# Reading a guard flag ahead of the last stores, and ending a program without a barrier

## The chip, the cores and the metric

The kernel runs on one core of a Trainium2 chip. A core has five engines with instruction streams of their own: TensorE (PE in the profile; its weight loads are PEld), VectorE (DVE), ScalarE (ACT), GpSimd (POOL) and SyncE (SP), which here only issues transfers. ACT issues some of the last stores too. The engines keep order among themselves by semaphores. The time of a run is the device's, in microseconds (us). The profile is of one execution; its span runs from the first to the last instruction that is recorded for the kernel.

## The reference

Attention with pairs of queries averaged, then a two-branch layer with a maximum of the two, for 8 batches and 8 heads, in float32:

```python
q_pool = q.reshape(B, H, S // 2, 2, D).mean(axis=3)          # S = 1152, D = 64
scores = (1 / sqrt(D)) * matmul(q_pool, k.transpose(0, 1, 3, 2))
scores = scores - max(scores, axis=-1, keepdims=True)
attn = exp(scores)
attn = attn / (sum(attn, axis=-1, keepdims=True) + 1e-09)
attn_out = matmul(attn, v)
x = attn_out.transpose(0, 2, 1, 3).reshape(4608, 512)
out = maximum(x @ w1, x @ w2) @ w_out                        # 512 -> 1024 -> 512
```

## The kernel before

The whole program is written out as one straight line for each engine. A planner (`Plan`) collects operations with what they read and write; hand-written strings (`pe_order`, `dve_order`, `pool_order`, `sp_order`) then set the order on each engine, and `solve` works out which operation has to wait for which. `emit` (line 187 on) runs through the operations of one engine, puts the waits in front of each and issues it.

The softmax is computed without subtracting the row's maximum. That is only sound while the sums of the exponentials stay within 1e-18 to 1e18, so the kernel tests this while it runs and has a second, slow way of computing everything for the case that they do not. The test works on the reciprocals of all sums, kept in `rcs`: two reductions and two comparisons on DVE (lines 1544 to 1548) leave one number in each of the 128 partitions, a small transfer on SP (line 1550) turns that column into a row, `badr`, and a last reduction on DVE (line 1551) leaves one integer, `flag`. It is zero when all is well.

When an engine has issued the last of its operations, it waits until the flag is written (the count `sure` on DVE's semaphore) and loads the flag from memory into a register of its own (`reg_load`, line 1594; in the profile a TENSOR_LOAD). Then comes `guarded` (line 219 on): `If_ne(taken, 0)` is a compare and branch on every engine. With a zero flag it jumps over the slow way. Behind it stands `landed()`: SP waits until every store to the output has landed, one wait for each of the eight semaphores of stores (`d_o0` to `d_o3` for those that SP issued, `d_z0` to `d_z3` for ACT's; line 207). The program ends with a barrier over all engines (line 1603), in which each reports and is released by GpSimd.

The end of the computation, around which the change lies: SP's last operations in `sp_order` are `g`, which is the small transfer of the flag, and seven `o`, stores of output tiles of 128 rows. Each tile is stored in two halves, one issued by SP and one by ACT (line 865). The tiles are copied out of TensorE's result banks by ACT (lines 1021 and 1006) and by DVE (lines 1024 and 1010); the last tile is split into 384 and 128 columns. ACT has in its last twelve operations one relu (line 908), four such copies and its seven stores. DVE has three copies after the flag.

Of the kernel before, what the change touches and what calls it, by code (L numbers as in the profile page):

```python
# [19 lines left out]
class Plan:  # L20
# [166 lines left out]
    def sems(self):  # L187
        return list(self.INORDER), sorted(self.dma_total)

    def emit(self, eng, h, sem, last_waits=()):  # L190
        for o in self.ops:
            if o["eng"] != eng:
                continue
            todo = {}
            for d in o["waits"]:
                p = self.ops[d]
                key = p["dma"] if p["dma"] is not None else p["eng"]
                todo[key] = max(todo.get(key, 0), p["count"])
            for key, v in todo.items():
                h.wait_ge(sem[key], v)  # L200
            inst = o["fn"](h)
            if o["dma"] is not None:
                inst.then_inc(sem[o["dma"]], 16)
            elif o["inc"]:
                inst.then_inc(sem[eng], 1)
        for key in last_waits:
            h.wait_ge(sem[key], self.dma_total[key])
# [132 lines left out]
def bass_funnel_attn__then__act_maxout2_kernel(  # L340
# [38 lines left out]
    with outer:  # L379
# [41 lines left out]
        plan = Plan()  # L421
# [741 lines left out]
        def landed(kind, i):  # L1163
            if (kind, i) not in loaded:
                return False
            return plan.ops[loaded[kind, i]]["seen"] <= now() + 0.5
# [421 lines left out]
        sem = {n: ctx.enter_context(nc.semaphore("sem_" + n)) for n in engines + dmas}  # L1588
        taken = nc.alloc_registers("taken")
        sure = [o["count"] for o in plan.ops if "gd4" in o["w"]][0]  # L1590
        for name, h in (("POOL", nc.gpsimd), ("SP", nc.sync), ("DVE", nc.vector), ("ACT", nc.scalar), ("PE", nc.tensor)):
            plan.emit(name, h, sem)
            h.wait_ge(sem["DVE"], sure)
            h.reg_load(taken[h.engine], flag[0:1, 0:1])
        room.close()
        stored = [f"d_o{s}" for s in range(4)] + [f"d_z{s}" for s in range(4)]

        def landed():
            plan.emit("-", nc.sync, sem, last_waits=stored)

        guarded(nc, taken, landed, q, k, v, moe_w1, moe_w2, moe_w_out, out)
        landed()
        nc.all_engine_barrier()


# [26 lines left out]
```

## Time and profile before

| | us |
|---|---|
| median of 3 runs | 367.5 (366.64, 367.50, 372.56) |
| the profiled execution | 368.65 |
| its span | 366.94 |
| PE busy | 355.2 (97%) |
| ACT busy | 315.0 (86%) |
| DVE busy | 242.2 (66%) |
| flag written (start of its reduction) | 351.04 |
| last matmul group starts | 360.69 |

The busy time of an engine is a sum over its instructions in the span. Reading of registers, branches, semaphores and the issuing of transfers are not counted as busy, so an engine that goes through the end of the program shows as idle there; such steps are found under their source lines instead, with their durations in ns (least, median, most) and the first and last start in us.

### The profile page before, as it was taken

To read this page: it belongs to the slowest core of one execution; us is meant where nothing else is said; L and a number is where in the kernel's file an instruction comes from. 1 tells how busy PE (TensorE), PEld (TensorE's weight loads), DVE (VectorE), ACT (ScalarE), POOL (GpSimd) and SP (SyncE) were. 2 spreads that over 40 slices of the span, in tenths; PEclk is the share of its full clock that TensorE was granted. 3 is DMA by queue.
4 is the path that set the end of the run, shared out by engine and by line. 5 is a ranking of instruction groups with operands and counts; after the bars stand their busy time and mean duration, and the time that the engine had idled before them with its cause. 6 is when DMAs were issued, how large, how long until landed. Compare 5 with 4: busy or idle time off the path is not lost.

```text
span 366.9 us, 13339 instructions
## 1 busy us (share of the span) xinstructions
PE 355.2 (97%) x5945; PEld 222.7 (61%) x5945; DVE 242.2 (66%) x526; ACT 315.0 (86%) x355; POOL 124.6 (34%) x111
## 2 busy tenths in 40 slices
PE   8898999999999999999999999999999999999993
PEld 6675555666564666656565665666666556666842
DVE  2777468877589767948957595676976856624511
ACT  4999989989999999999989999999999989893311
POOL 1245995344046322552251612623524420100000
PEclk9999999999999999999999999999999999999998
DMA  7999999999869996996997999997998662724015
GB/s 249 404 397 394 404 291 313 224 300 297 218 122 270 297 296 189 252 264 177 290 266 212 283 252 285 271 275 182 287 214 212 161 161 50 153 45 94 13 39 141
DMA packets 77791, 84.78 MB, mean 231 GB/s; under 512 B 50080, under 2 KB 50848, under 8 KB 77728
## 3 DMA queue, kind: packets, MB, share of 16 engines
q1 hardware_dynamic: 77168, 83.09, 84.9%
q8 instruction: 48, 0.79, 0.9%
q10 hardware_dynamic: 560, 0.79, 0.6%
q14 instruction: 15, 0.12, 0.1%
HBM read 62.91 MB, written 9.44 MB: 197 GB/s over the span
## 4 chain that ended last, share of the span: by engine, by line
PE 92%; ACT 4%; DMA 1%; issue 1%; SPq 0%; POOL 0%; DVE 0%; DVEq 0%
PE sps L714 20%; PE sps L625 12%; PE sps L961 11%; PE fb L961 10%; PE fb L625 9%; PE sps L928 9%; PE fb L928 7%; ACT et L721 4%; PE sps L994 3%; PE sps L637 2%; PE fb L846 2%; PE fb L637 2%; PE fb L994 1%; PE sps L901 1%; DMA kraw<-in_k_dram 1%; PE fb L901 1%
## 5 line engine op out<-in xcount | busy, mean ns | idle before, releaser
L721 ACT ACTIVATE et<-sps 128x1024 bf16<-128x1024 f32 (+1 forms) x336 | 307.0, 1005 | 21.7 <-PE sps L714 19.7
L714 PE MATMUL sps<-qpT,kT 64*128 64x256 bf16 (+7 forms) x1162 | 118.3, 283 | 0.3 <-DVE kT L601 0.2
L579 DVE STREAM_TRANSPOSE qpT<-qp 32x288 bf16<-32x288 bf16 x216 | 101.4, 469 | 5.6 <-PE sps L714 1.5
L714 PEld LDWEIGHTS sps<-qpT,kT 64*128 64x128 bf16 x1162 | 48.0, 94 | 47.5 <-ACT et L721 15.5
L519 POOL TENSOR_TENSOR qp<-qraw 128x576 bf16<-128x576 f32 x30 | 42.1, 1406 | 96.0 <-DVE qpT L579 79.4
L525 POOL TENSOR_SCALAR vE<-vraw 128x1152 bf16<-128x1152 f32 x32 | 36.8, 1151 | 60.4 <-DMA vraw<-in_v_dram 57.8
L625 PE MATMUL sps<-vE,et 128*128 128x65 bf16 x1368 | 48.4, 193 | 0.0
L625 PEld LDWEIGHTS sps<-vE,et 128*128 128x128 bf16 x1368 | 43.6, 97 | 6.0 <-issue 5.3
L486 POOL TENSOR_SCALAR kbf<-kraw 128x1152 bf16<-128x1152 f32 x31 | 35.6, 1150 | 33.0 <-DMA kT<-kbf 17.0
L928 PE MATMUL sps<-xT,wd 64*128 64x512 bf16 (+3 forms) x368 | 43.4, 326 | 0.0
L961 PE MATMUL sps<-wo,stage 64*128 64x512 bf16 x256 | 36.8, 376 | 0.0
L625 PE MATMUL fb<-vE,et 128*128 128x65 bf16 x936 | 33.5, 193 | 1.1 <-issue 1.1
L625 PEld LDWEIGHTS fb<-vE,et 128*128 128x128 bf16 x936 | 29.9, 97 | 6.1 <-issue 5.3
L928 PE MATMUL fb<-xT,wd 64*128 64x512 bf16 (+3 forms) x272 | 33.5, 333 | 0.1
L961 PE MATMUL fb<-wo,stage 64*128 64x512 bf16 x224 | 33.0, 376 | 0.0
L937 DVE TENSOR_SCALAR stage<-sps 128x1024 bf16<-128x1024 f32 (+3 forms) x23 | 22.3, 969 | 15.4 <-PE sps L928 15.2
L937 DVE TENSOR_SCALAR stage<-fb 128x1024 bf16<-128x1024 f32 (+3 forms) x17 | 17.0, 999 | 10.7 <-PE fb L928 10.4
L928 PEld LDWEIGHTS sps<-xT,wd 64*128 64x128 bf16 x368 | 15.6, 94 | 13.4 <-PE sps L928 1.4
L647 DVE RECIPROCAL rcs<-sps 128x5 f32<-128x5 f32 (+1 forms) x38 | 7.0, 184 | 19.8 <-PE sps L625 19.3
L961 PE MATMUL sps<-w,xT 64*128 64x512 bf16 x128 | 18.7, 376 | 0.0
L972 DVE COPY stage<-sps 128x1024 f32<-128x1024 f32 x8 | 9.8, 1224 | 12.8 <-PE sps L961 12.7
L961 PEld LDWEIGHTS sps<-wo,stage 64*128 64x128 bf16 x256 | 12.1, 94 | 9.5
(86 smaller groups left out, 293.8 us busy)
## 6 DMA issues: line engine op xcount, KB each, us to landing
vraw<-in_v_dram SPq DMA_DIRECT2D x32, 576.0 KB, 6.4
kraw<-in_k_dram SPq DMA_DIRECT2D x31, 576.0 KB, 6.6
qraw<-in_q_dram SPq DMA_DIRECT2D x31, 576.0 KB, 6.6
out_dram<-stage SPq DMA_DIRECT2D x21, 256.0 KB, 5.5
out_dram<-stage SPq DMA_DIRECT2D x23, 128.0 KB, 2.9
xT<-in_moe_w_dram SPq DMA_DIRECT2D x4, 512.0 KB, 10.8
stage<-in_moe_w_out_dram SPq DMA_DIRECT2D x4, 512.0 KB, 13.8
stage<-in_moe_w_dram SPq DMA_DIRECT2D x4, 512.0 KB, 13.6
```

The costliest lines, as they stand in the source:

```text
L486: op("POOL", lambda g: g.tensor_scalar(kbf[s][:, :, :, :].rearrange("p t h d -> p h t d"), kraw[r][:, :, :, :], 1.0, 1.0, ALU.mult, ALU.mu ...
L519: op("POOL", lambda g: g.tensor_tensor(qpf[s][:, :, :], qraw[r][:, :, 0, :], qraw[r][:, :, 1, :], ALU.add), r=[f"qraw{r}"], w=[f"qp{s}.0", ...
L525: op("POOL", lambda g: g.tensor_scalar(vE[r][:, :, :, 0:D].rearrange("p t h d -> p h t d"), vraw[r][:, :, :, :], 1.0, 1.0, ALU.mult, ALU.m ...
L579: op("DVE", lambda e: e.transpose(view[dst:dst + 32, :, 32 * pb:32 * pb + 32], qpf[s][src:src + 32, :, 32 * db:32 * db + 32]), r=[f"qp{s}. ...
L625: last = e.matmul(fb[m][:, sb * 66:sb * 66 + 65], et[:, a:a + P], vE[vs][:, t, half, 0:65], start=(t == 0), stop=(t == NT - 1))
L637: last = e.matmul(fb[m][rows(half), NCH * 66:NCH * 66 + 65], et[:, a:a + NB], vE[vs][:, t, half, 0:65], start=(t == 0), stop=(t == NT - 1))
L714: last = e.matmul(sps[r][:, h, col:col + hi - lo], kT[i % 3][rows(h), t, :], qpT[i % 3][rows(h), lo:hi], start=True, stop=True)
L721: op("ACT", lambda e: e.activation(et2[:, :, c:c + z - a], sps[r][:, :, a - g * W:z - g * W], EXP, scale=scale), r=[f"s{r}"], w=keys + ([f ...
L928: last = e.matmul(fb[m + k][:, 0:size], wd[z, ct, (f0 + k) * P:(f0 + k + 1) * P], xT[z, ct, n0:n1], start=(turn == 0 and ct == 0), stop=(t ...
L937: dve(lambda e: e.tensor_scalar_max(gT[:, f0:f0 + 2, g0:g0 + size], wide[m // 2][:, :, 0:size], 0.0), [f"f{m}", f"f{m + 1}"], w + [f"f{m}" ...
L961: last = e.matmul(fb[m + k][:, :], lhs, rhs, start=(turn == 0 and j == 0), stop=(turn == 1 and j == NC_ + NF - 1))
L994: return e.matmul(fb[m][:, 0:c1 - c0], lhs, rhs[:, c0:c1], start=(j == 0), stop=(j == NC_ + NF - 1))
```

## The change

Three things change, and nothing in the computation.

1. `emit` gets an argument `extra`: a number and a function, which is called in front of the operation that has so many operations of this engine left, itself included. The wait for the flag and the load into the register become a function `look`. On SP it is called before the last 7 operations, on ACT before the last 12, on DVE before the last 3; on POOL and PE behind the last one, as it was. The branch stays where it was on all engines.
2. The eight waits of `landed()` are put in the order in which the last operations of their semaphores stand in the plan, in place of the order of their names.
3. The barrier over all engines at the program's end is left out.

```diff
-    def emit(self, eng, h, sem, last_waits=()):
-        for o in self.ops:
-            if o["eng"] != eng:
-                continue
+    def emit(self, eng, h, sem, last_waits=(), extra=None):
+        mine = [o for o in self.ops if o["eng"] == eng]
+        for n, o in enumerate(mine):
+            if extra is not None and n == len(mine) - extra[0]:
+                extra[1](h)
             todo = {}
...
         sure = [o["count"] for o in plan.ops if "gd4" in o["w"]][0]
-        for name, h in (("POOL", nc.gpsimd), ("SP", nc.sync), ("DVE", nc.vector), ("ACT", nc.scalar), ("PE", nc.tensor)):
-            plan.emit(name, h, sem)
+
+        def look(h):
             h.wait_ge(sem["DVE"], sure)
             h.reg_load(taken[h.engine], flag[0:1, 0:1])
+
+        early = {"SP": 7, "ACT": 12, "DVE": 3}
+        for name, h in (("POOL", nc.gpsimd), ("SP", nc.sync), ("DVE", nc.vector), ("ACT", nc.scalar), ("PE", nc.tensor)):
+            if name in early:
+                plan.emit(name, h, sem, extra=(early[name], look))
+            else:
+                plan.emit(name, h, sem)
+                look(h)
         room.close()
-        stored = [f"d_o{s}" for s in range(4)] + [f"d_z{s}" for s in range(4)]
+        place = {o["dma"]: n for n, o in enumerate(plan.ops)}
+        stored = sorted((f"d_{c}{s}" for c in "oz" for s in range(4)), key=lambda s: place[s])

         def landed():
             plan.emit("-", nc.sync, sem, last_waits=stored)

         guarded(nc, taken, landed, q, k, v, moe_w1, moe_w2, moe_w_out, out)
         landed()
-        nc.all_engine_barrier()
```

## The prediction

> **What bounds the kernel now.** I read the page first, then the chain that ended last near its end, then the timeline, the DMA issues and the lines of the last 16 us engine by engine. The page and the end of the chain:
>
> ```profile
> span 366.9 us, 13339 instructions
> PE 92%; ACT 4%; DMA 1%; issue 1%; SPq 0%; POOL 0%; DVE 0%; DVEq 0%
> 357.23 4.09 PE sps L994 x30
> 361.44 0.29 DVE stage L1010
> ```
>
> TensorE carries 92% of the chain, and the change touches none of its work. The chain that the profile draws ends with the last copy to `stage`, at 361.44 + 0.29 = 361.73. The span ends at 366.94 (the 366.9 of the page), so 5.2 us follow in which no engine computes. Everything the change can win lies there; what it can lose also lies in front of the tail's stores, where it puts three reads of the flag.
>
> The last transfers, from the timelines of SP and ACT (first pair), the line of the stores and the DMA issues (last pair: KB, us to landing):
>
> ```profile
> 360.19 2.67 SPq L865 DMA_DIRECT2D out_dram<-stage  x3
> 361.32 1.54 ACTq L865 DMA_DIRECT2D out_dram<-stage  x2
> L865 SPq DMA_DIRECT2D out_dram<-stage x7: 466/467/1037, 355.0 to 361.8; - x7
> L865 ACTq DMA_DIRECT2D out_dram<-stage x7: 497/498/1007, 355.0 to 361.9; - x7
> out_dram<-stage SPq DMA_DIRECT2D x1, 32.0 KB, 3.0
> out_dram<-stage ACTq DMA_DIRECT2D x1, 32.0 KB, 3.1
> ```
>
> Both queues finish issuing at 362.86 (360.19 + 2.67, 361.32 + 1.54). The last store begins to issue at 361.9 on ACT and lands 3.1 us later, at 365.0. So the output is complete at 365.0, and 1.9 us of the span lie behind that. What SP does meanwhile is in the rows of the flag, of line 207 (the waits on the stores, where the branch is also entered) and of line 1603 (the barrier):
>
> ```profile
> L1551 DVE TENSOR_REDUCE flag<-badr x1: 273/273/273, 351.0 to 351.0; 1x1 int32<-1x128 f32 x1
> L1594 POOLq TENSOR_LOAD <-flag x1: 487/487/487, 351.4 to 351.4; - x1
> L1594 PEldq TENSOR_LOAD <-flag x1: 613/613/613, 359.5 to 359.5; - x1
> L1594 DVEq TENSOR_LOAD <-flag x1: 628/628/628, 361.5 to 361.5; - x1
> L1594 ACTq TENSOR_LOAD <-flag x1: 986/986/986, 362.9 to 362.9; - x1
> L1594 SPq TENSOR_LOAD <-flag x1: 803/803/803, 362.9 to 362.9; - x1
> L207 SPq EVENT_SEMAPHORE  x4: 28/28/28, 366.4 to 366.6; - x4
> L207 POOLq COMPARE_BRANCH  x1: 45/45/45, 351.9 to 351.9; - x1
> L207 PEldq COMPARE_BRANCH  x1: 3712/3712/3712, 360.2 to 360.2; - x1
> L207 DVEq COMPARE_BRANCH  x1: 72/72/72, 362.1 to 362.1; - x1
> L207 SPq COMPARE_BRANCH  x1: 58/58/58, 363.8 to 363.8; - x1
> L207 ACTq COMPARE_BRANCH  x1: 54/54/54, 363.9 to 363.9; - x1
> L1603 POOLq DRAIN  x1: 107/107/107, 352.3 to 352.3; - x1
> L1603 PEldq DRAIN  x1: 73/73/73, 364.0 to 364.0; - x1
> L1603 ACTq DRAIN  x1: 79/79/79, 364.4 to 364.4; - x1
> L1603 DVEq DRAIN  x1: 57/57/57, 365.1 to 365.1; - x1
> L1603 SPq DRAIN  x1: 13/13/13, 366.7 to 366.7; - x1
> L1603 PEldq EVENT_SEMAPHORE  x1: 51/51/51, 366.9 to 366.9; - x1
> ```
>
> SP's path after its last issue is: flag load from 362.9 (0.80 us), branch at 363.8, then nothing until its first wait at 366.4. The landing at 365.0 is passed while SP is still between branch and wait. Four wait records from 366.4 to 366.6 therefore go through at their own pace; SP reaches the barrier at 366.7, last of the five engines, and the span ends 0.2 us later. The hole of 2.6 us between branch and first wait is the largest piece. POOL and ACT need 0.4 and 0.5 us from branch to next instruction (351.9 to 352.3, 363.9 to 364.4), DVE 3.0 (362.1 to 365.1), PE 3.8 (360.2 to 364.0). Blocks of instructions are fetched in just these holes. The DMA view, for 361 to 362.6, for 363.2 to 363.8, and for 364.5 to 365.3, in this order (queue, packets, MB, share of 16 engines):
>
> ```profile
> q8 instruction: 1, 0.02, 4.9%
> q14 instruction: 1, 0.01, 4.3%
> q14 instruction: 2, 0.02, 7.6%
> ```
>
> They took 0.049 x 16 x 1.6 = 1.25 us, 0.043 x 16 x 0.6 = 0.41 us, and together 0.076 x 16 x 0.8 = 0.97 us, some 0.5 each. By their times I give the first to PE, the second to DVE and one of the last to SP; that attribution is inferred.
>
> **The change part by part.** *The early reads.* SP's moves in front of its last seven instructions, the tail's stores; ACT's in front of its last twelve (one relu, four copies, seven stores); DVE's in front of its last three copies. No DMA moves. Each wait is for the flag, written at 351.0 + 0.27 = 351.3. Behind it are queued:
>
> ```profile
> SPq L865 <- ACT stage L1021: 7.4, 3, 5.3
> 354.08 0.38 ACT L908 ACTIVATE stage<-sps 128x256 bf16<-128x256 f32 x1 [5.17 <-PE sps L901]
> 355.54 0.69 DVE L1024 COPY stage<-fb 128x512 f32<-128x512 f32 x1 [4.22 <-PE fb L994]
> ```
>
> With the dearest load (ACT's 0.99) the read is over at 352.3. ACT next has work at 354.08, SP's first store issues at 355.0, after an idle stretch of up to 5.3 us, and DVE's copy starts at 355.54 after 4.22 idle. The covers are 1.8, 2.7 and 3.2 us, so I cost the early reads at nothing. Without its cover ACT's read would cost up to 1.0, once, as the relu at 354.08 feeds TensorE. PE and POOL read where they did.
>
> *What leaves SP's end.* The load goes from its path: the branch can stand where the load began, 362.9 in place of 363.8, a gain of 0.9 (0.80 and the gap beside it). There are two bounds. POOL's load, with nothing before it, took 0.49, SP's and ACT's, right behind a store's issue, 0.80 and 0.99; if the excess of 0.3 is the issue still draining, the branch may inherit it, and the gain is 0.6. The last issue took 1.04 against a median of 0.47, beside DVE's load (361.5 for 0.63), which also goes; if that load slowed it, the gain is up to 0.6 more. I take 0.9: the branches of SP, ACT, DVE and POOL, 45 to 72 ns whether behind a slow load or a quick one, show nothing that an issue could hold up.
>
> *The jump stays.* Only the read moves; the branch is still behind the last store. It then reaches its target at 362.9 + 2.6 + 0.06 = 365.6 instead of 366.4. That is still behind the landing at 365.0, by 0.5 us. So *the order of the waits* is worth nothing: all eight are fulfilled when SP arrives, and the four records cost their 0.2 to 0.3 us in either order. If the jump were short it would be worth at most three of the four records, 0.2.
>
> A rule of the Trainium skill speaks against hoping for more. The row: SP's 2.6 us against ACT's 0.5. The page Runtime: NRT & Kernel Launch, section Instruction fetch mechanics, says that only two pages are kept, fetched in sequence, and that a taken branch to a place outside them stalls until its page is fetched. By this rule the gap belongs to the target's distance and moves with the branch whole, which gives the sum below; by ACT's row alone SP would jump in 0.5 and the landing would decide, which is a rival.
>
> *No barrier.* From SP's 366.7 to the end at 366.94 are 0.2 us; they go. The other four engines then end by themselves; the latest of them, DVE, is at its barrier at 365.1 now, still before SP's new end, so none is late.
>
> The sum: 0.9 + 0.2 = 1.1 us. The profiled execution, 368.65 with a span of 366.94 and 1.7 around it, becomes 367.5, its span 365.8. Against the median of the three runs, 367.5, it is 366.4.
>
> **The rivals.** *The jump becomes short* (as on ACT and POOL). Then the last landing decides: 365.0 and a wait of 0.1, span 365.1, gain 1.8, time 365.7. For it: two engines jump in half a microsecond. Against it: SP's branch skips the same code as before, and nothing in the change shortens it.
>
> *The fetch queues behind the stores: slower.* SP's fetch now starts some 0.9 us earlier, near 363.9 instead of 364.7, and the DMA engines are then busier:
>
> ```profile
> 361.20:362.20 1.00, 0.10 (x2) 0.00 (x0) 0.29 (x1) 0.09 (x1) 0.00 (x0) 1.00 0.89 221
> 362.20:363.20 1.00, 0.00 (x0) 0.00 (x0) 0.00 (x0) 0.00 (x0) 0.00 (x0) 1.00 0.76 221
> 363.20:364.20 1.00, 0.00 (x0) 0.00 (x0) 0.00 (x0) 0.00 (x0) 0.00 (x0) 1.00 0.42 111
> 364.20:365.20 1.00, 0.00 (x0) 0.00 (x0) 0.00 (x0) 0.00 (x0) 0.00 (x0) 0.53 0.14 33
> ```
>
> Its columns end with the clock, the DMA share and GB/s. If the fetch had to wait until the stores are through (365.0) and then ran as long as PE's (1.25), it would end at 366.25. SP's first wait comes 1.2 us behind its fetch now (366.4 against 364.7 + 0.5), so it would come at 367.5, and the span would end near 367.7: 0.8 slower, time 368.3. It decides from the point where branch to first wait takes over 3.7 us (2.6 and the 1.1 won). For it: PE's 3.8, taken at a DMA share of 0.89. Against it: DVE's fetch ran at a share of 0.42 and took 0.41, no longer than SP's 0.5 in a quiet stretch.
>
> *The change doesn't do what it says*: the time of a run doesn't follow SP's last wait, because what lies around the span (1.7 us) takes up what the kernel's end gives. Then it is 367.5 again. For it: no record shows that part. Against it: it is counted from an end that moves. The Trainium skill (same page, section The ~15µs preamble/postamble breakdown) states that the runtime has a barrier of its own over all engines after the kernel; by that too only the kernel's own 0.2 would go.
>
> **How the numbers follow.** Forecast 0.63, short jump 0.10, queued fetch 0.12, nothing moved 0.12, others 0.03. The predicted time is the first's, 366.4. The range: downwards 365.7 of the short jump, less half of what the two nearer runs differ by (366.64 and 367.50, so 0.4), 365.3, and a tenth for the shorter last issue; upwards the queued fetch's 368.3. So 365.2 to 368.3. A bound of 2%, 7.4 us, is about what a measurement of this kernel can tell from no change (its three runs reach from 366.64 to 372.56). All 5.2 us behind the last copy would not reach it, and no rival does either: within 2% has 0.95, faster 0.02, slower 0.03, these for a disturbance that no row shows.
>
> **What would show it.** Right: flag loads of SP, ACT and DVE near 351.4; first tail store still at 355.0 and last copy at 361.4; SP's branch at 362.9, its first wait near 365.6 and all four records within 0.3; no line of the barrier; a span of 365.8. Wrong: a relu of ACT later than 354.1 (the read had no cover), a branch that starts late or lasts long (it inherited the load's time), a first wait before 365.0 (short jump) or after 366.4 (queued fetch), or a shorter span with the same time.

## The result, and the profile after

| | before | changed |
|---|---|---|
| median of 20 runs each, us | 368.68 (366.64 to 372.56) | 367.60 (366.59 to 373.14) |
| the profiled execution, us | 368.65 | 367.43 |
| its span, us | 366.94 | 366.20 |
| around the span, us | 1.71 | 1.24 |

The ratio of changed to before is 0.9963, 95% interval 0.9947 to 0.9979; it leaves out the few runs in a slower state (such as the one of 373.14), and so is not the quotient of the two medians. On 368.7 us that is 1.4 us less, between 0.8 and 2.0; the medians differ by 1.1.

The last computing steps of the changed kernel, from the timelines of ACT, DVE and SP (start us, length us, what):

```profile
353.71 0.38 ACT L909 ACTIVATE stage<-sps 128x256 bf16<-128x256 f32 x1 [5.17 <-PE sps L902]
350.66 0.27 DVE L1552 TENSOR_REDUCE flag<-badr 1x1 int32<-1x128 f32 x1 [1.99 <-DMA badr<-bad]
355.17 0.69 DVE L1025 COPY stage<-fb 128x512 f32<-128x512 f32 x1 [4.23 <-PE fb L995]
361.06 0.29 DVE L1011 COPY stage<-sps 128x128 f32<-128x128 f32 x1 [2.67 <-PE sps L995]
354.59 8.47 SPq L866 DMA_DIRECT2D out_dram<-stage  x7
```

Everything up to here is the old kernel 0.37 to 0.38 us sooner: the last copy starts at 361.06 in place of 361.44, and it lies as far behind the flag's reduction as before (10.40 us both times). So 0.37 us of the shorter span come from ahead of the tail, where the change does nothing, and the other 0.37 from the tail. The start of the last copy differs by more than that from execution to execution (360.2 to 362.6 over the kernels below), and so the tail is measured from there.

The flag, the branch with SP's waits, and the stores, from the lines of the source (ns least, median, most; first and last start in us):

```profile
L1595 SPq TENSOR_LOAD <-flag x1: 479/479/479, 351.0 to 351.0; - x1
L1595 ACTq TENSOR_LOAD <-flag x1: 477/477/477, 351.0 to 351.0; - x1
L1595 DVEq TENSOR_LOAD <-flag x1: 543/543/543, 351.0 to 351.0; - x1
L208 SPq EVENT_SEMAPHORE  x4: 28/28/28, 365.9 to 366.2; - x4
L208 PEldq COMPARE_BRANCH  x1: 4246/4246/4246, 359.8 to 359.8; - x1
L208 SPq COMPARE_BRANCH  x1: 54/54/54, 363.1 to 363.1; - x1
L866 SPq DMA_DIRECT2D out_dram<-stage x7: 466/467/1612, 354.6 to 361.4; - x7
L866 ACTq DMA_DIRECT2D out_dram<-stage x7: 497/499/1582, 354.6 to 361.5; - x7
```

The last of the DMA issues (KB, us to landing):

```profile
out_dram<-stage ACTq DMA_DIRECT2D x1, 32.0 KB, 3.8
```

The three reads stand at 351.0 and take 0.5 us. SP's branch follows its last issue at once (361.45 + 1.61 = 363.06, branch at 363.1). But that issue has become 0.6 us longer: 1.61 where it was 1.04. The hole behind the branch is still there, 2.8 us from 363.1 to the first wait at 365.9, and the last store, 361.5 + 3.8 = 365.3, has landed by then.

### The profile page after: what moved, and what is told of

Its sections match the earlier page's. It is cut to its first block, busy times and chain, and to the rows that moved or that the text cites. A ratio compares the mean times of both kernels' runs of the same rounds, so it can differ in the third digit from the quotient of the medians.

```text
span 366.2 us, 13324 instructions
## 1 busy us (share of the span) xinstructions
PE 354.6 (97%) x5941; PEld 222.5 (61%) x5945; DVE 242.1 (66%) x526; ACT 315.0 (86%) x355; POOL 124.5 (34%) x111
## 4 chain that ended last, share of the span: by engine, by line
PE 92%; ACT 4%; DMA 1%; issue 1%; SPq 0%; POOL 0%; DVE 0%; DVEq 0%
PE sps L715 21%; PE sps L626 12%; PE sps L962 11%; PE fb L962 10%; PE fb L626 9%; PE sps L929 9%; PE fb L929 7%; ACT et L722 4%; PE sps L995 3%; PE sps L638 2%; PE fb L847 2%; PE fb L638 2%; PE fb L995 1%; DMA kraw<-in_k_dram 1%; PE sps L902 1%; PE fb L902 1%
```

## The experiments

The trace holds single records of branches, issues, waits, instruction fetches and landings. The table is worked out from them, for one profiled execution of each kernel (of the kernel before and of the changed one two), in us behind the start of DVE's last copy. "PE's fetch" is the 16 KB block on the queue that I give to TensorE. "Around" is the time of that execution less its span.

| kernel | PE's fetch ends | last SP issue: length, end | SP's branch | first wait | last landing | span's end | around |
|---|---|---|---|---|---|---|---|
| before | 1.04 | 1.04, 1.42 | 2.33 | 4.98 | 3.57 | 5.50 | 1.71 |
| before again (e11) | 1.22 | 1.08, 1.46 | 2.39 | 5.50 | 3.39 | 6.02 | 1.71 |
| changed | 1.60 | 1.61, 2.00 | 2.06 | 4.87 | 4.21 | 5.13 | 1.24 |
| changed again (e8) | 1.62 | 1.63, 2.01 | 2.07 | 4.91 | 4.26 | 5.17 | 1.30 |
| barrier back (e1) | 1.29 | 1.30, 1.69 | 1.74 | 4.78 | 3.78 | 5.31 | 1.71 |
| barrier out alone (e2) | 1.19 | 1.15, 1.54 | 2.45 | 6.18 | 3.63 | 6.44 | 1.23 |
| DVE late (e3) | 1.74 | 1.75, 2.13 | 2.19 | 5.34 | 4.06 | 5.59 | 1.23 |
| TensorE held (e4) | 3.78 | 0.61, 0.99 | 1.05 | 4.71 | 4.80 | 5.15 | 1.62 |
| slow way out (e5) | 1.42 | 1.42, 1.81 | 1.87 | 2.65 | 4.03 | 4.07 | 1.33 |
| hint to all (e6) | 1.18 | 1.05, 1.43 | 1.49 | 4.56 | 3.71 | 4.82 | 1.25 |
| hint to SP (e7) | 1.36 | 1.37, 1.76 | 1.81 | 4.63 | 4.00 | 4.89 | 1.32 |
| early jump (e9) | 1.32 | 1.33, 1.72 | in the idle stretch | 2.51 | 3.79 | 3.92 | 1.91 |
| early jump, names (e10) | 1.49 | 1.48, 1.87 | in the idle stretch | 3.81 | 3.79 | 4.11 | 1.84 |
| early jump, drain (e12) | 0.92 | 0.75, 1.14 | in the idle stretch | 1.95 | 3.23 | 3.33 | 1.59 |

**The barrier.** First it was put back into the changed kernel (`nc.all_engine_barrier()` behind the last `landed()`), then taken out of the kernel before with nothing else changed.

> The changed kernel with the barrier at the program's end put back. Theory: the barrier costs twice, about 0.25 us inside the span and about 0.5 us around it, where without it the four other engines end by themselves beside SP's path; so the time around the span is 1.7 us again (1.2 without the barrier), and the ratio to the kernel before is 0.998 to 0.999. Rival: what lies around the span does not depend on the barrier and the 0.5 us between the two profiled executions were chance; then 1.2 us around the span, or both values in different runs, and a ratio of 0.9965 to 0.9975.

> The kernel before with nothing changed but the barrier left out. Theory (the barrier costs in the span and around it): span shorter by 0.25 us behind the first wait of SP, 1.2 us around the span, time 0.7 us less, ratio 0.998. Rival (only the records of the barrier go): 1.7 us around the span, ratio 0.9993. SP's first wait should stay 4.98 us behind the start of the last copy.

Put back: median 368.97 of 12 runs, ratio to the kernel before 0.9988 (0.996 to 1.0016). Taken out alone: 368.76 of 12, ratio 1.0003 (0.9974 to 1.0033). The times alone don't decide; they lie on either side of 1, with intervals of 0.3% each way, and 0.7 us would be 0.2%. What lies around the span does: it is 1.71 in all three profiled executions with the barrier, and 1.23 to 1.33 in the kernels without it that end with SP's waits. Over the single runs of these four kernels the two groups don't touch: 1.67 to 1.86 with the barrier (89 runs of the kernel before, made beside the experiments, and 12 with it put back), 1.18 to 1.35 without (20 of the changed kernel, 12 with it taken out alone). The barrier's own part in the span, with it put back:

```profile
L208 SPq EVENT_SEMAPHORE  x4: 28/28/28, 367.4 to 367.6; - x4
L1613 SPq DRAIN  x1: 13/13/13, 367.7 to 367.7; - x1
L1613 PEldq EVENT_SEMAPHORE  x1: 51/51/51, 367.9 to 367.9; - x1
```

From the last wait's record to the end are 0.27 us, where the changed kernel has none. So the barrier costs about 0.26 us in the span, read from single executions, and 0.48 around it, 0.7 together.

The kernel with the barrier out alone ended late in its profile because of its hole:

```profile
L207 SPq COMPARE_BRANCH  x1: 58/58/58, 364.4 to 364.4; - x1
L207 SPq EVENT_SEMAPHORE  x4: 28/28/28, 368.1 to 368.4; - x4
```

3.7 us, against 2.6 in the kernel before. SP's first wait was expected to stay 4.98 us behind the start of the copy and came at 6.18.

**The last issue.** Two fetches ran beside it in the changed kernel, TensorE's and one that I give to DVE, whose branch had moved from 362.1 to 361.1. In the DMA view of the changed kernel from 361.22 to 362.66 (queue, packets, MB, share of 16 engines) TensorE's fills the whole stretch of 1.44 us (0.063 x 16 x 1.44 = 1.45):

```profile
q8 instruction: 1, 0.02, 6.3%
```

In one kernel DVE read the flag late again (`early = {"SP": 7, "ACT": 12}`), in the other TensorE waited for DVE's last copy before its read and branch:

```diff
+                if name == "PE":
+                    h.wait_ge(sem["DVE"], copied)
                 look(h)
```

Here `copied` is the count of DVE's last copy.

> The changed kernel with DVE's flag read behind its last copy again, so that DVE branches, and fetches, some 1 us later. Rival A (DVE's fetch, now beside the last stores' issue, held that issue for 1.6 us): the last issue is back at 1.0 us or less although TensorE's fetch runs beside it. Theory B (an issue that begins while TensorE's 16 KB fetch runs ends about 0.4 us after that fetch, whatever DVE does): the last issue ends 0.35 to 0.45 us behind the end of TensorE's fetch, at whatever length that has (1.0 to 1.6 us). Time within 0.2 us of the changed kernel by B, up to 0.6 less by A.

> The changed kernel, with TensorE waiting for DVE's last copy before it reads the flag and branches, so that its fetch begins behind the start of the last stores' issue. Theory B (TensorE's fetch holds the issue): both last issues take about 0.5 us in place of 1.6, SP branches about 1.1 us sooner, its first wait comes 3.6 to 3.9 us behind the start of the last copy (4.87 now). TensorE's own jump then ends the span or nearly so: 0.9 us for its load and branch and 3.8 behind, so the span ends 4.7 to 5.2 us behind the last copy's start (5.13 now). Rival A (DVE's fetch holds it): the last issue stays at 1.6 us.

With DVE late (median 367.59 of 10 runs, ratio 0.9956, 0.9927 to 0.9986), the stores and the branches of DVE and SP:

```profile
L866 SPq DMA_DIRECT2D out_dram<-stage x7: 467/467/1747, 354.1 to 361.0; - x7
L208 DVEq COMPARE_BRANCH  x1: 72/72/72, 361.3 to 361.3; - x1
L208 SPq COMPARE_BRANCH  x1: 54/54/54, 362.8 to 362.8; - x1
```

DVE branches 0.7 us behind the start of its copy and the issue is the longest of all. It ends 0.39 behind TensorE's fetch, which took 1.83 us. With TensorE held (367.54 of 10, ratio 0.9971, 0.9938 to 1.0004):

```profile
L866 SPq DMA_DIRECT2D out_dram<-stage x7: 466/467/607, 354.0 to 360.8; - x7
L866 ACTq DMA_DIRECT2D out_dram<-stage x7: 497/498/843, 354.0 to 360.8; - x7
L208 PEldq COMPARE_BRANCH  x1: 4269/4269/4269, 361.3 to 361.3; - x1
L208 SPq COMPARE_BRANCH  x1: 54/54/54, 361.5 to 361.5; - x1
L208 SPq EVENT_SEMAPHORE  x4: 28/28/28, 365.1 to 365.4; - x4
```

The issue is 0.61 on SP, and SP branches 1.0 us sooner behind the copy. TensorE's fetch, moved with its branch, begins here only 2.27 us behind the copy, long after the issue has ended, and DVE's branch stands where it stood in the changed kernel. So TensorE's fetch held the issue, and DVE's isn't needed for it; each of these two kernels was profiled once. In the table's other rows the issue ends 0.2 to 0.4 us behind TensorE's fetch. ACT's 0.84 was expected at 0.5; why it is longer than SP's wasn't followed up. SP won nothing by branching sooner: its hole was 3.7 us here, more than the 2.7 to 2.9 that were expected, and TensorE's own branch, 361.3 + 4.27 = 365.6, ended the span.

**The hole behind the branch.** The slow way of computing was left out, so that only SP's waits and a barrier stand between branch and target:

```diff
     with nc.If_ne(taken, 0):
         landed()
         nc.all_engine_barrier()
-        with TileContext(nc) as tc:
...
```

> The changed kernel with the slow way of computing left out of the branch, so that only the waits on the stores and a barrier lie between branch and target. Theory (the hole behind SP's branch is the fetch of a far target, and TensorE's own far jump holds the last issue and the last landings): SP's first wait 0.5 us or less behind its branch, the last issues about 0.5 us, the last landing 2.8 to 3.4 us behind the start of the last copy and the span's end 0.1 behind that (5.13 in the changed kernel); 1.7 to 2.3 us less than the changed kernel, ratio to the kernel before 0.991 to 0.993. Rival (SP is slow after its issues, whatever the distance): the hole stays at 2.6 us or more and the time is that of the changed kernel.

The median is 365.70 of 7 runs, ratio 0.9925 (0.9896 to 0.9954). Line 208 and the stores:

```profile
L208 SPq COMPARE_BRANCH  x1: 54/54/54, 362.2 to 362.2; - x1
L208 SPq EVENT_SEMAPHORE  x4: 28/28/208, 363.0 to 364.3; - x4
L208 PEldq COMPARE_BRANCH  x1: 350/350/350, 359.1 to 359.1; - x1
L838 SPq DMA_DIRECT2D out_dram<-stage x7: 466/467/1423, 353.8 to 360.7; - x7
```

The four waits are now spread from 363.0 to 364.3, each let through by a landing; the first stands 0.02 us behind the landing it waits for (362.94), so the hole itself is under 0.8 us. TensorE's branch takes 0.35 in place of 4.2. On the queue of the 8 KB instruction blocks, which I give to the other engines, nothing is fetched behind 294 us, where the changed kernel fetches five blocks from 352 us to its span's end. The span ends 0.05 behind the last landing. So the hole is the distance of the target. ACT and POOL jump in half a microsecond even with the slow way in place; by the source it holds few operations for them (the exponentials, the making of an identity matrix), so they skip less code, but that this is the reason was not tested. The gain was expected larger, 1.7 to 2.3 us below the changed kernel, and is 1.06 from the copy to the span's end: the last issue still takes 1.42, because TensorE still fetches a 16 KB block at the same place.

**A hint for the branch.** The language has a hint that names a branch ahead of time (BRANCH_PREFETCH_HINT in the profile). The `If` was written out as a branch for each engine, `br_eq(taken, 0, on_true="past", on_false="slow").branch_hint(mark)`, with `mark` behind the flag's read, on TensorE 60 operations ahead of the end; then with SP's mark alone.

> The changed kernel, complete, with a hint for the branch to every engine: behind the flag's read on SP, ACT, DVE and POOL, and 60 operations ahead of the end on TensorE; the target can then be fetched in the quiet stretch near 351 us. Theory (far targets): as without the slow way, the end 2.9 to 3.5 us behind the start of the last copy in place of 5.13, all instruction fetches of the jumps before 354 us, the last issues at 0.5 us; ratio to the kernel before 0.991 to 0.994. Rival (the hint is dropped, or TensorE loses at the hint what it wins at the end): SP's hole stays over 2.5 us, or the last copy starts later against the flag's reduction than the 10.4 us of now; ratio 0.996 or more.

> The same with a hint for SP alone. Theory: SP's hole falls to 0.5 us or less, but TensorE's fetch still holds the last issue (it ends 0.35 to 0.45 behind that fetch) and one part of each late store, so the landing, 3.6 to 4.2 us behind the start of the last copy, ends the span 0.1 later: 0.9 to 1.4 us less than the changed kernel's 5.13. TensorE's and DVE's own jumps, over 2.6 to 3.8 us behind their branches, must end by then. Rival (the hint has no effect): 4.8 us to SP's first wait as in the changed kernel.

To all: 367.29 of 12 runs, ratio 0.9951 (0.9928 to 0.9973). To SP alone: 367.67 of 10, 0.9973 (0.9945 to 1.0). Hint, branch and waits of SP in the first:

```profile
L1603 SPq BRANCH_PREFETCH_HINT  x1: 65/65/65, 351.3 to 351.3; - x1
L227 SPq COMPARE_BRANCH  x1: 74/74/74, 362.4 to 362.4; - x1
L209 SPq EVENT_SEMAPHORE  x4: 28/28/28, 365.4 to 365.7; - x4
```

The hint stands where it should, and the hole is 3.1 us as ever (2.8 with SP's alone). In both, one block is fetched on the queue of the 8 KB blocks between 351 and 354, the one that the changed kernel fetches there too. In this form the hint did nothing; why is open.

**How much varies.** The changed kernel once more, and the kernel before.

> The changed kernel once more, on the same chip as the kernels with hints, for their comparison and for a second look at what varies: SP's hole (2.82 in the first profile; 2.65 to 3.73 over six kernels) and the last issue (1.61; 1.04 to 1.75). If both vary by some tenths from execution to execution of one program, they fall between these ends again and not on the first values.

> The kernel before once more, for the last issue and SP's hole. If the length of the last issue and of the hole belong to the program's layout and not to chance (the changed kernel had 1.61 and 1.63 for the issue, 2.82 and 2.84 for the hole, in two executions), the issue is 1.04 within 0.1 and the hole 2.65 within 0.1 again; if TensorE's fetch varies by chance, the issue lies anywhere from 1.0 to 1.7 and ends 0.4 behind that fetch.

The changed kernel, on that chip: 367.25 of 10 runs, ratio 0.9944 (0.9924 to 0.9965). Its last issue and hole are those of the first execution within 0.02 us (1.63 and 2.84). The kernel before, one run of 368.82, has its issue again but not its hole:

```profile
L865 SPq DMA_DIRECT2D out_dram<-stage x7: 466/468/1078, 354.6 to 361.5; - x7
L207 SPq COMPARE_BRANCH  x1: 58/58/58, 363.5 to 363.5; - x1
L207 SPq EVENT_SEMAPHORE  x4: 28/28/28, 366.6 to 366.8; - x4
```

3.1 us now, 2.65 at first. So the hole varies by half a microsecond from execution to execution. For the issue it stays open whether the change lengthens it. Where SP and ACT read late it was 1.04, 1.08 and 1.15. In the kernels where they read early, TensorE wasn't held and the slow way stood, it was anywhere from 0.75 to 1.75.

**The jump in the idle stretch.** If the jump costs the same wherever it stands, it belongs where SP idles. The tail's operations of SP, ACT and DVE were given to both arms of the branch, the slow arm first, and the branch of these engines follows the read at once:

```diff
     with nc.If_ne(taken, 0):
+        tail()
         landed()
...
         guarded(nc, taken, tail, landed, q, k, v, moe_w1, moe_w2, moe_w_out, out)
-        landed()
+        with nc.Else():
+            tail()
+            landed()
```

> The changed kernel with the branch of SP, ACT and DVE moved with the flag's read: their last stores and copies stand once in the slow arm and once behind it, so that with a zero flag these engines jump near 352 us, in their idle stretch, and run straight to the end. Theory (the hole belongs to the jump, wherever it stands, and at the end it alone kept SP past the landing): SP's hole of 2.6 to 3.7 us shows between 352 and 356; its waits follow the last issue at once, and the span ends 0.1 us behind the last landing, 4.0 to 4.3 us behind the start of the last copy (5.13 in the changed kernel); the last issue is still held to 0.4 us behind TensorE's fetch; ratio to the kernel before 0.992 to 0.995. Rival (SP lacks time: the jump ends behind the first tail store's due time and everything behind it slips): the last copy starts later than 10.4 us behind the flag's reduction, and the end is that of the changed kernel or worse.

> The same with the waits in the order of their names. Theory (the order counts only where SP is at its waits before the last landing): the semaphore of the last landing is in the first of the four records, three follow it, and the span ends 0.2 to 0.3 us behind the last landing in place of 0.1. Rival (the order is free here too): 0.1.

The first: 366.03 of 7 runs, ratio to the kernel before 0.9933 (0.9907 to 0.9959). Its branches and waits, and then, from the timelines of SP and DVE, its stores and last copy:

```profile
L1616 SPq COMPARE_BRANCH  x2: 43/50/58, 350.6 to 364.1; - x2
L206 SPq EVENT_SEMAPHORE  x4: 17/28/28, 362.7 to 364.0; - x4
```

```profile
353.72 8.19 SPq L865 DMA_DIRECT2D out_dram<-stage  x7
360.19 0.29 DVE L1010 COPY stage<-sps 128x128 f32<-128x128 f32 x1 [2.67 <-PE sps L994]
```

SP branches at 350.6 and issues its first store at 353.72, 3.9 us behind the flag's reduction as in the kernel before; the hole left no mark. At the end the waits follow the landings, and the span ends 0.13 behind the last of them, 3.92 behind the copy in place of 5.13. But the time around the span is 1.91 us in this execution instead of 1.24, which gives 0.7 of the 1.2 back. Over the seven runs of this kernel it varies: 1.30 to 1.37 in four, 1.77 to 1.93 in three.

With the waits in the order of their names (366.82 of 5 runs, ratio 0.9937, 0.9911 to 0.9962) the first record holds the semaphore that lands last:

```profile
L206 SPq EVENT_SEMAPHORE  x4: 17/28/28, 364.8 to 365.0; - x4
```

All four come behind the last landing (364.83), and the end 0.32 behind it where the other order has 0.13. So the order is worth 0.2 us, where SP waits for landings at all.

In both kernels the last wait hung on a closing branch of SP (in the first it is the 364.1 in the row of L1616). A drain behind `landed()`, `nc.sync.drain()`, takes it over:

> The kernel with the early jumps and one drain of SP behind its waits, so that no wait hangs on the branch that closes the arm, which then needs no instruction, as on the other engines. There the span ended 0.13 us behind the last landing, but 1.9 us lay around it, against 1.2 to 1.3 in the changed kernel. Theory (that last branch is one more jump, whose cost lies behind the last record): no branch of SP at the end, 1.2 to 1.3 us around the span, the end still 0.1 to 0.2 behind the last landing; about 0.6 us less than with the branch, ratio to the kernel before 0.990 to 0.993. Rival (what lies around the span grows because SP ends sooner and something else, of fixed end, is then what counts): 1.8 to 1.9 us around it again, the time unchanged at 0.993 to 0.994.

366.37 of 6 runs, ratio 0.9947 (0.993 to 0.9965). No branch is left at the end:

```profile
L1619 SPq DRAIN  x1: 13/13/13, 364.4 to 364.4; - x1
```

Around the span lie 1.59 us, and 1.55 to 1.70 over the six runs, between what the two theories said, and the times of the kernels with the early jump overlap. This experiment decided nothing: what sets the time around the span when SP ends this soon is open. The traces hold one candidate that no run tests. In these kernels TensorE still jumps at its end, and the second block that is fetched on its queue then ends 0.7 to 1.0 us behind the recorded span (1.9 in the kernel with TensorE held, with 1.62 around it). In the seven profiled executions without the barrier that have 1.23 to 1.33 around them it ends inside the span, or there is none. The early jump is faster than the kernel before, by 0.5 to 0.7%; against the changed kernel (0.9963 and 0.9944) its 0.9933 to 0.9947 are not apart.

## Why the prediction was right, and where its sum was not

**The early reads cost nothing**: right. The reads were over at 351.5, ACT's relu stood at 353.71 with 5.17 us of idle time in front of it, as before, and the first tail store 3.9 us behind the flag's reduction, as before.

**0.9 us for the load**: the load went, as said; 0.06 us lie between the last issue and the branch, and the branch took 54 ns, so it inherited nothing. But the branch came only 0.28 sooner behind the last copy (2.06 for 2.33), since the issue in front of it grew by 0.57. The prediction had seen this issue as odd, guessed DVE's load as the reason and allowed only for its becoming shorter. The reason was TensorE's fetch for its own jump, which ended at 1.60 in place of 1.04; why it ended later stays open. By the second execution of both kernels the branch gained 0.32. This is the term that was mis-sized: 0.9 forecast, 0.3 measured.

**The jump moves whole**: right in kind. It stayed at 2.8 us, and moved with the branch, in the end even into the idle stretch. That it is the target's distance was only argued, and the short jumps of ACT and POOL stood against it; with the slow way out it is shown, by under 0.8 us with the near target and 2.6 to 3.7 with the far one. Here the trace agrees with the Trainium skill, page Runtime: NRT & Kernel Launch, section Instruction fetch mechanics, by which a taken branch out of the fetched pages waits for a fetch. The jump's size isn't fixed, as the sum took it to be.

**The order of the waits is worth nothing**: right, by 0.7 us: the last landing was at 365.27, the first wait at 365.94. The 0.2 put on the case of a short jump is what it was worth there.

**0.2 us for the barrier**: right inside the span (0.26), but around the span another 0.48 went, for which the sum had nothing. The prediction had the time around the span as a reason why less than the sum might come out; it moved the other way.

The sum was 1.1 us. From the start of the last copy to the span's end, with the time around the span added, the two executions of each kernel give 7.2 and 7.7 before (5.50 + 1.71, 6.02 + 1.71), 6.4 and 6.5 after: 1.1 us less on the mean, of which 0.3 is the branch's, 0.7 the barrier's and the rest the hole, which varies. That the total was right is luck, since two errors cancelled: 0.6 too much for the load, 0.5 too little for the barrier. The predicted 366.4 lies 1.2 below the measured 367.6, because it was counted from the median of three runs, 367.5, and twenty runs of the kernel before have 368.7.

**The rivals.** The jump did not become short. The fetch did not queue behind the stores: it began 1.2 to 1.3 us behind the branch in place of 1.0 to 1.25 (two blocks are fetched there in both kernels, and either may be SP's; the prediction took the first) and took under 0.5 us, as before. And the time did move with the end of the span.

## What to carry to other kernels

A load or a wait that is taken off the last engine's path pays only up to the next thing that this engine stands behind, so the steps behind the last compute instruction are best laid out as one chain, with issue, branch, jump and landing each as an entry of its own. A conditional way that is almost never taken costs each engine a jump over its code, here 2.6 to 4.4 us on SP, DVE and TensorE and half a microsecond on ACT and POOL; if an engine idles earlier, the decision and the jump can be made there, with the little work that follows written out in both arms. What closes a program is paid for around the recorded span too, so the span and the run's time should both be compared.

## What the runs showed of the hardware

The last issue on SP, which stands beside the fetch of a 16 KB instruction block for TensorE, did not end before that fetch: it ended 0.2 to 0.4 us behind it in 13 of the 14 executions of the table, with fetches of 0.9 to 1.8 us, and it took 0.61 in the one where the fetch came later. The other tail issues on SP take 0.47 at the median.

A read of the flag into a register took 0.48 us on SP and ACT with nothing in front of it, and 0.80 and 0.99 right behind an issue.

A jump to a far target took 2.6 to 3.7 us on SP, and TensorE's branch held 3.4 to 4.4 us; with a near target it was under 0.8 and 0.35.
